# Mask and row maxima in one VectorE pass, and a new operation list with less work on GpSimd, in a fused attention and two-layer kernel

## The chip, the cores and the metric

The program runs on one core of a Trainium2 chip. The metric is the device time of one execution in microseconds (us); the profile adds one traced execution. The engines are called PE (TensorE, with PEld for its weight loads), DVE (VectorE), ACT (ScalarE), POOL (GpSimd) and SP (SyncE, which here only issues DMAs). A matrix product runs on PE, everything around it on DVE, ACT and POOL, and each engine works through its own queue strictly in order.

## The reference

Three stages follow one another on 1536 tokens (2 batches of 768) of width 512. First an attention with 8 heads of 64: each query sees the keys within 15 positions and, over all positions, 24 block keys (the maximum over blocks of 32) with block means as values. Then a gated layer of width 1536 behind an RMS norm, and a layer of width 2048 with ELU.

```python
k_sum = k.reshape(B, H, nb, 32, D).max(axis=3)
v_sum = v.reshape(B, H, nb, 32, D).mean(axis=3)
scores_l = np.where(mask_l, scale * q @ k.T, -1e9)          # |i - j| < 16
scores_s = scale * einsum('bhsd,bhnd->bhsn', q, k_sum) + log(32)
a = softmax(concat([scores_l, scores_s]), eps=1e-9)
x = a @ concat([v, v_sum])
xn = x / rms(x) * rms_g
x = (silu(xn @ w_gate) * (xn @ w_val)) @ w_out
out = elu(x @ w_in) @ w_out2
```

## The kernel before

**Tiles.** Attention is cut into 12 head-wise "pairs" of query tiles, (batch, j) with j = 0 to 5; each covers 128 queries and yields two tiles, (b, j, h) with h = 0, 1, of 128 rows by 4 head pairs by 120 columns (96 window keys and 24 block keys). A tile goes through `scores` (PE), mask, row maxima, `exps` (ACT, four exponentials with row sums), `guard` (row sum + 1e-9), `invert`, `normalize`, `turn_e` (PE transposes), `copy_e` and `apply_v2` (PE). For the first four pairs (eight tiles) PE adds the mask itself (`premask`), the keys are copied with the scale in them (`copy_keys`), and DVE takes only the row maxima. For the other eight pairs (16 tiles) DVE first scales the scores and adds the mask (`add_mask`) and then takes the row maxima of the result (`row_max`), each over 128x480.

**Layers.** The token axis is cut in three blocks of 512. Products run on float pairs: a weight tile `ws_*` or `wd` and an activation are split into a rounded high part (`split_a`, `act_a`: a cast on ACT) and a low part (`split_b`, `act_b`: a subtraction), and each product takes three matmuls of 512 columns. The weights arrive packed; `convert_a`, `convert_l` and `convert_b` unpack them on ACT and DVE. Block 0 goes through both layers directly while attention for the other two blocks proceeds; blocks 1 and 2 then share a seven-product scheme (`up_product`, `down_product`), which fills the rest of the time.

**Order.** Nothing is scheduled at run time. `add` records each operation with the engines that may do it, and `PLAN` lists all operations in the order of issue: a number is four times the operation's place in the record plus the choice of engine. `TAGS` chooses PSUM banks. So the queue of each engine, and of the DMAs on SP, is written out by hand. Before the first scores PE runs dummy matmuls on zeros (`keep_warm`), some of which wait for a key tile to land.

**POOL** in the old list has 55 operations: masks and zeros, four roots (`root`), six `normalize`, three `copy_keys`, four copies of the block means into value windows (`repeat_v`), two `add_square`, and 24 `split_b` and five `act_b` of 128x512.

Of the kernel before, what the change touches and what calls it, by code (L numbers as in the profile page):

```python
# [20 lines left out]
P = 128  # L21
# [30 lines left out]
def fused_kernel(ctx: ExitStack, tc: tile.TileContext, q, k, v, w_gate, w_val, w_out, rms_g, w_in2, w_out2, out):  # L52
# [342 lines left out]
    def add_place(b, due, gap):  # L395
        add({ACT: 0.72, DVE: 0.6} if b == 0 else {ACT: 0.8, DVE: 0.85}, 0, due, place_v, b, r=[f"vm{b}" if b else f"vp{b}"], w=["va0#s"])
        for i in range(1, VA):
            add({POOL: 0.6, ACT: 0.52} if b == 0 else {POOL: 0.6}, 0, due + gap * i, repeat_v, i, r=["va0#s"], w=[f"va{i}#s"])
# [18 lines left out]
    def copy_keys(eng, b, t):  # L417
        factor = scale if b * NQ + t < PRE else 1.0
# [47 lines left out]
    def add_mask(b, t, var):  # L466
        nc.vector.scalar_tensor_tensor(
            T[f"e{b}_{t}"], T[f"s{b}_{t}"], scale, masks[var].unsqueeze(1).to_broadcast([P, NP, NK]), op0=ALU.mult, op1=ALU.add)
# [4 lines left out]
    def exps(b, t, pre):  # L473
        e = T[f"e{b}_{t}"]
        s, nm = T[f"s{b}_{t}"] if pre else e, T[f"nm{b}_{t}"]
        ss = new("ss", f"ss{b}_{t}", [P, NP])
        for pr in range(NP):
            nc.scalar.activation(  # L478
                out=e[:, pr, :], in_=s[:, pr, :], func=AF.Exp, bias=nm[:, pr:pr + 1],
                accum_out=ss[:, pr:pr + 1])  # L480

    def guard(b, t):
        ss = T[f"ss{b}_{t}"]
        nc.vector.tensor_scalar_add(ss, ss, 1e-9)
# [47 lines left out]
    def add_pair(b, j, due, tags):  # L532
# [4 lines left out]
        for t in (2 * j, 2 * j + 1):  # L537
            lo, hi, _ = window(t)
            if b * NQ + t >= MT:
                add_window(b, t, due - 3)  # L540
            near = [f"kT{b}_{x}" for x in range(lo // (2 * P), (hi - 1) // (2 * P) + 1)]
            add({POOL: 0.86, DVE: 0.45, ACT: 0.65}, 0, due, copy_keys, b, t,
                r=near + far, w=[f"ka{b}_{t}"], new=[("ka", f"ka{b}_{t}")])
# [9 lines left out]
        for h, n in enumerate(ns):  # L553
            at = due + 0.6 * h
            src = f"s{n}"
            if not pre:
                add(DVE, 0.56, at + 1.4, add_mask, b, f"{j}_{h}", mask_of(j), r=[f"s{n}", f"mask{mask_of(j)}"], w=[f"e{n}"])
                src = f"e{n}"
            add(DVE, 0.56, at + 1.9, row_max, b, f"{j}_{h}", src, r=[src], w=[f"nm{n}"], new=[("nm", f"nm{n}")])
            add(ACT, 1.43 if pre else 1.5, at + 2.6, exps, b, f"{j}_{h}", pre, r=[f"nm{n}"] + [f"s{n}", f"pm{n}"] * pre,  # L560
                w=[f"e{n}", f"ss{n}"], new=[("ss", f"ss{n}")])
            add(DVE, 0.13, at + 4, guard, b, f"{j}_{h}", w=[f"ss{n}"])
            add(DVE, 0.1, at + 4, invert, b, f"{j}_{h}", r=[f"ss{n}"], w=[f"rs{n}"], new=[("rs", f"rs{n}")])
            add({POOL: 0.94, DVE: 0.58, ACT: 1.14}, 0, at + 4.3, normalize,
# [22 lines left out]
    def add_square(eng, blk, cs, i):  # L587
        s = T[f"sq{blk}_{SQ[blk][0]}{i}"]
        (nc.gpsimd if eng == POOL else nc.vector).tensor_add(s, s, T[f"sq{blk}_{cs}{i}"])
# [61 lines left out]
    def add_norm(blk, lo, hi, due, tag):  # L651
# [5 lines left out]
        for n, cs in enumerate(SQ[blk]):  # L657
# [3 lines left out]
            if n >= n_sums:  # L661
                add({POOL: 1.28, DVE: 0.6}, 0, due + 0.6 * n, add_square, blk, cs, i, r=[sq], w=[first])
# [92 lines left out]
    def add_act(src, dst, due, tag="act"):  # L755
        h, l = dst + "h", dst + "l"
        add(ANY_SB, 0, due, act_a, src, dst, tag, r=[src], w=[h], new=[(tag, h)])
        add(ANY_2[1], 0, due + 0.6, act_b, src, dst, tag, r=[src, h], w=[l], new=[(tag, l)])
# [463 lines left out]
    def keep_warm(i):  # L1222
# [3 lines left out]
        for _ in range(WARM_LONG.get(i, 2)):  # L1226
# [6 lines left out]
    for i, at in enumerate(WARM_AT):  # L1233
        add(PE, 0.44, at, keep_warm, i, r=[f"kT0_{AFTER_K[i]}"] if i in AFTER_K else [], new=[(BANKS, f"warm{i}")])
# [245 lines left out]
```

## Time and profile before

| | us |
|---|---|
| median of 3 runs (591.71 to 592.02) | 591.72 |
| the profiled execution's own time | 592.67 |
| its span, first to last instruction | 591.0 |
| PE busy | 574.1 (97%) |
| DVE busy | 547.3 (93%) |
| ACT busy | 430.4 (73%) |
| POOL busy | 69.6 (12%) |

The profiled execution lasted 1.67 us longer than its span and 0.95 us longer than the median run. Busy times are unions of the instructions' intervals; neighbouring instructions overlap, so the time from one start to the next is shorter than the mean duration that a view prints.

### The profile page before, as it was taken

How to read it: one execution, taken by the hardware profiler on the slowest of the kernel's cores; microseconds unless marked ns; L12 is line 12 of the kernel's file. 1: busy time of each engine (PE TensorE's matmuls, PEld its weight loads, DVE VectorE, ACT ScalarE, POOL GpSimd, SP SyncE). 2: the span in 40 equal slices, each digit the busy share in tenths (PEclk: the TensorE clock that was granted, in tenths of full speed). 3: DMA queues.
4: the chain of work that ended last, by engine and by line, in shares of the span. 5: the costliest groups of instructions: out<-in, count | busy, mean ns of one | idle time of the engine just before them, and what ended most of it. 6: DMA issues, size and time to landing. Idle time of an engine off the chain costs nothing.

```text
span 591.0 us, 9948 instructions
## 1 busy us (share of the span) xinstructions
PE 574.1 (97%) x3366; PEld 467.6 (79%) x3366; DVE 547.3 (93%) x1049; ACT 430.4 (73%) x953; POOL 69.6 (12%) x89
## 2 busy tenths in 40 slices
PE   7799989999999999999999999999999999999997
PEld 3588768788877888888888888888888888888886
DVE  5999999999989988989998999999999999999993
ACT  3889978998988988646534456676666989788750
POOL 3326425024100031100000000000000000000000
PEclk9999999999999999999999999999999999999999
DMA  8888889988978977142134416324316552742202
GB/s 318 287 297 280 303 303 321 325 300 282 312 231 273 318 232 265 55 159 71 55 91 161 143 50 188 92 81 142 107 38 196 200 159 78 244 129 65 71 35 107
DMA packets 56051, 108.79 MB, mean 184 GB/s; under 512 B 6784, under 2 KB 19584, under 8 KB 56000
## 3 DMA queue, kind: packets, MB, share of 16 engines
q1 hardware_dynamic: 56000, 108.16, 56.2%
q8 instruction: 26, 0.43, 0.3%
q14 instruction: 25, 0.20, 0.1%
HBM read 79.82 MB, written 28.31 MB: 183 GB/s over the span
## 4 chain that ended last, share of the span: by engine, by line
PE 81%; DVE 9%; ACT 6%; issue 2%; DMA 1%; POOL 0%; DVEq 0%; ACTq 0%; POOLq 0%
PE acc L766 11%; PE B_1u L937 8%; PE ph L710 7%; PE C_1u L937 6%; PE A_1u L937 6%; PE B_2d L1116 6%; PE B_2u L937 6%; PE B_1d L1116 4%; PE C_2d L1116 4%; PE A_2d L1116 4%; PE C_2u L937 4%; PE A_2u L937 4%; PE C_1d L1116 3%; PE A_1d L1116 3%; PE pg L710 2%
## 5 line engine op out<-in xcount | busy, mean ns | idle before, releaser
L710 PE MATMUL ph<-xa,ws_i 128*128 128x512 f32 x192 | 48.0, 395 | 0.6 <-DVE ex L747 0.6
L937 PE MATMUL B_1u<-xh,w_1u 128*128 128x512 f32 x144 | 47.8, 391 | 0.0
L710 PEld LDWEIGHTS ph<-xa,ws_i 128*128 128x128 f32 x192 | 35.5, 188 | 8.8 <-DVE ex L747 1.0
L710 PE MATMUL pg<-xs,ws_g 128*128 128x512 f32 (+1 forms) x168 | 36.4, 364 | 0.7 <-DVE th L734 0.7
L1116 PE MATMUL B_2d<-td,wd 128*128 128x512 f32 x144 | 34.6, 389 | 0.0
L146 DVE TENSOR_TENSOR wd<-rd,wd 128x512 fp32r<-128x512 f32 x49 | 32.8, 684 | 0.2 <-ACT wd L135 0.2
L937 PE MATMUL C_1u<-xh,w_1u 128*128 128x512 f32 x96 | 32.8, 390 | 0.0
L710 PEld LDWEIGHTS pg<-xs,ws_g 128*128 128x128 f32 x168 | 28.1, 189 | 5.5 <-DVE th L734 0.9
L937 PE MATMUL A_1u<-xh,w_1u 128*128 128x512 f32 x96 | 32.3, 390 | 0.0
L135 ACT CAST wd<-rd 128x512 fp32r<-128x512 f32 x49 | 29.1, 621 | 4.1 <-PE B_2u L937 2.2
L937 PEld LDWEIGHTS B_1u<-xh,w_1u 128*128 128x128 f32 x144 | 27.0, 188 | 6.1 <-ACT h_1u L135 0.3
L937 PE MATMUL B_2u<-xh,w_2u 128*128 128x512 f32 x96 | 31.6, 389 | 0.0
L1116 PEld LDWEIGHTS B_2d<-td,wd 128*128 128x128 f32 x144 | 27.0, 188 | 5.6
L937 PE MATMUL B_1u<-xl,w_1u 128*128 128x512 f32 x72 | 28.1, 390 | 0.0
L1116 PE MATMUL B_1d<-td,wd 128*128 128x512 f32 x108 | 26.5, 389 | 0.0
L478 ACT ACTIVATE e<-e,nm 128x120 f32<-128x120 f32 x64 | 24.5, 387 | 1.7 <-DVE nm L471 1.6
L135 ACT CAST td<-z 128x512 fp32r<-128x512 f32 x28 | 17.1, 619 | 11.7 <-DVE z L1098 11.6
L1116 PE MATMUL C_2d<-td,wd 128*128 128x512 f32 (+1 forms) x102 | 24.5, 377 | 0.0
L1116 PE MATMUL A_2d<-td,wd 128*128 128x512 f32 x96 | 24.0, 389 | 0.0
L1116 PEld LDWEIGHTS B_1d<-td,wd 128*128 128x128 f32 x108 | 20.3, 188 | 4.2
L135 ACT COPY h_1u<-B_1u 128x512 f32<-128x512 f32 x21 | 12.3, 587 | 12.9 <-PE B_1u L937 12.9
L937 PE MATMUL C_2u<-xh,w_2u 128*128 128x512 f32 x64 | 21.5, 389 | 0.0
(547 smaller groups left out, 1777.2 us busy)
## 6 DMA issues: line engine op xcount, KB each, us to landing
st_i<-in_moe_w_in SPq DMA_DIRECT2D x16, 512.0 KB, 4.4
st_p<-in_moe_w_out SPq DMA_DIRECT2D x16, 512.0 KB, 4.9
st_v<-in_moe_w_val SPq DMA_DIRECT2D x12, 512.0 KB, 6.8
st_g<-in_moe_w_gate SPq DMA_DIRECT2D x12, 512.0 KB, 6.1
st_o<-in_moe_w_out SPq DMA_DIRECT2D x12, 512.0 KB, 5.7
kept_i<-raw_i SPq DMA_DIRECT2D x16, 256.0 KB, 4.3
kept_p<-raw_p SPq DMA_DIRECT2D x16, 256.0 KB, 4.4
va<-in_v SPq DMA_DIRECT2D x20, 192.0 KB, 5.8
```

Source lines behind the costliest of these rows:

```text
L135: nc.scalar.copy(out=out, in_=in_)
L146: (nc.gpsimd if eng == POOL else nc.vector).tensor_sub(out, a, b)
L478: nc.scalar.activation(out=e[:, pr, :], in_=s[:, pr, :], func=AF.Exp, bias=nm[:, pr:pr + 1], accum_out=ss[:, pr:pr + 1])
L710: nc.tensor.matmul(pt[:, i], wt[:, a, kk * P:(kk + 1) * P], xt[:, c, i], start=(kk == 0 and n == 0), stop=(kk == KM - 1 and n == 2))
L766: nc.tensor.matmul(acc, wt[:, a, cs], ot[e], start=(first and n == 0), stop=(last and n == 2))
L937: nc.tensor.matmul(pt, wt[:, a, cs], xt[e][:, kk], start=first and kk == n == 0, stop=kk == 1 and n == 2, skip_group_check=not first)
L1116: nc.tensor.matmul(pt[:, h], wt[:, a, cs], xt[:, e, h], start=first and n == 0, stop=last and n == 2 and h.stop == TB, skip_group_check=i ...
```

## The change

For the 16 tiles of the later eight pairs, `add_mask` and `row_max` become four `tensor_tensor_reduce` instructions, one for each head pair (128x120): each adds the mask to the scores, multiplies by -1, writes the negated result and puts its minimum into `nm`. `exps` then exponentiates -1 times what was written. The scale is now in the copied keys of all pairs. On POOL remain masks, zeros and roots, six `normalize` and one `copy_keys` of the early pairs, and it gets 11 of the 24 `guard`. The 24 `split_b`, five `act_b` and two `add_square` go to DVE, `repeat_v` goes to DVE (five) and ACT (one), and 12 copies and squares go from DVE to ACT. The dummy matmuls keep their number (22 of 512 columns) but come in 11 short operations instead of eight, one of which had eight matmuls in a row. `PLAN` and `TAGS` are new from the first number to the last (2819 operations instead of 2832), so all engines' queues and SP's order of DMAs change.

```diff
     def add_place(b, due, gap):
...
         for i in range(1, VA):
-            add({POOL: 0.6, ACT: 0.52} if b == 0 else {POOL: 0.6}, 0, due + gap * i, repeat_v, i, r=["va0#s"], w=[f"va{i}#s"])
+            add({DVE: 0.34, ACT: 0.52}, 0, due + gap * i, repeat_v, i, r=["va0#s"], w=[f"va{i}#s"])
...
     def copy_keys(eng, b, t):
-        factor = scale if b * NQ + t < PRE else 1.0
+        factor = scale
...
     def add_mask(b, t, var):
-        nc.vector.scalar_tensor_tensor(
-            T[f"e{b}_{t}"], T[f"s{b}_{t}"], scale, masks[var].unsqueeze(1).to_broadcast([P, NP, NK]), op0=ALU.mult, op1=ALU.add)
+        e, x, nm = T[f"e{b}_{t}"], T[f"s{b}_{t}"], new("nm", f"nm{b}_{t}", [P, NP])
+        for pr in range(NP):
+            nc.vector.tensor_tensor_reduce(
+                e[:, pr, :], x[:, pr, :], masks[var], -1.0, 3.0e38, ALU.add, ALU.min, nm[:, pr:pr + 1])
...
-                out=e[:, pr, :], in_=s[:, pr, :], func=AF.Exp, bias=nm[:, pr:pr + 1],
+                out=e[:, pr, :], in_=s[:, pr, :], func=AF.Exp, bias=nm[:, pr:pr + 1], scale=1.0 if pre else -1.0,
                 accum_out=ss[:, pr:pr + 1])
-    def guard(b, t):
+    def guard(eng, b, t):
         ss = T[f"ss{b}_{t}"]
-        nc.vector.tensor_scalar_add(ss, ss, 1e-9)
+        (nc.gpsimd if eng == POOL else nc.vector).tensor_scalar_add(ss, ss, 1e-9)
...
-            add({POOL: 0.86, DVE: 0.45, ACT: 0.65}, 0, due, copy_keys, b, t,
+            add({POOL: 0.86, DVE: 0.45, ACT: 0.65} if early else {DVE: 0.45, ACT: 0.65}, 0, due, copy_keys, b, t,
...
-            add(DVE, 0.13, at + 4, guard, b, f"{j}_{h}", w=[f"ss{n}"])
+            add({DVE: 0.13, POOL: 0.25}, 0, at + 4, guard, b, f"{j}_{h}", w=[f"ss{n}"])
...
-            add({POOL: 0.94, DVE: 0.58, ACT: 1.14}, 0, at + 4.3, normalize,
+            add({POOL: 0.94, DVE: 0.58, ACT: 1.14} if early else {DVE: 0.58, ACT: 1.14}, 0, at + 4.3, normalize,
...
-    def add_square(eng, blk, cs, i):
+    def add_square(blk, cs, i):
         s = T[f"sq{blk}_{SQ[blk][0]}{i}"]
-        (nc.gpsimd if eng == POOL else nc.vector).tensor_add(s, s, T[f"sq{blk}_{cs}{i}"])
+        nc.vector.tensor_add(s, s, T[f"sq{blk}_{cs}{i}"])
...
-        add(ANY_2[1], 0, due + 0.6, act_b, src, dst, tag, r=[src, h], w=[l], new=[(tag, l)])
+        add(ANY_2[0], 0, due + 0.6, act_b, src, dst, tag, r=[src, h], w=[l], new=[(tag, l)])
...
-        for _ in range(WARM_LONG.get(i, 2)):
+        for _ in range(2):
...
 PLAN = (
...
-WARM_AT = (3.4, 3.9, 4.0, 7.5, 8.5, 9.5, 10.5, 13.0)
-AFTER_K, WARM_LONG = {1: 0, 2: 2}, {1: 8}
+WARM_AT = (3.4, 3.9, 4.0, 7.5, 8.5, 9.5, 10.5, 13.0, 7.8, 8.0, 8.2)
+AFTER_K = {1: 0, 2: 2, 8: 0, 9: 1, 10: 1}
 ACT_B = 0
-LO_0, LO_1 = (1, 1, 1), 0
+LO_0, LO_1 = (0, 0, 0), 0
```

## Rows read from the trace of the kernel before

**Rows 1.** Windows of 15 us: busy time of each engine, granted clock, DMA share.
```profile
0.00:15.00 15.00, 10.86 (x74) 5.24 (x78) 8.19 (x25) 5.70 (x19) 4.70 (x29) 1.00 0.87 321
15.00:30.00 15.00, 11.53 (x257) 8.97 (x250) 14.39 (x41) 13.24 (x63) 5.90 (x8) 1.00 0.85 282
30.00:45.00 15.00, 13.88 (x205) 12.52 (x206) 14.85 (x36) 13.46 (x32) 3.44 (x4) 1.00 0.87 302
45.00:60.00 15.00, 14.34 (x93) 12.86 (x92) 14.93 (x30) 14.53 (x44) 9.34 (x10) 1.00 0.88 284
60.00:75.00 15.00, 13.86 (x143) 10.82 (x145) 14.59 (x24) 12.56 (x32) 7.93 (x7) 1.00 0.87 300
75.00:90.00 15.00, 13.27 (x109) 9.88 (x99) 13.61 (x27) 12.75 (x33) 2.34 (x3) 1.00 0.87 296
...
375.00:390.00 15.00, 15.00 (x68) 12.42 (x67) 15.00 (x27) 10.92 (x21) 0.00 (x0) 1.00 0.23 67
```
**Rows 2.** The page's chain that ended last, by engine.
```profile
PE 81%; DVE 9%; ACT 6%; issue 2%; DMA 1%; POOL 0%; DVEq 0%; ACTq 0%; POOLq 0%
```
**Rows 3.** Timeline of PE, 4 to 18 us: start, us, instruction, count, wait.
```profile
7.03 1.05 PE L1227 MATMUL warm<-idle_w 128*128 128x512 bf16 x2
...
8.16 3.00 PE L1227 MATMUL warm<-idle_w 128*128 128x512 bf16 x8
...
11.38 1.05 PE L462 MATMUL s<-ka,q 64*64 64x120 f32 x32
...
14.76 1.05 PE L462 MATMUL s<-ka,q 64*64 64x120 f32 x32 [1.65 <-DVE ka L143]
15.74 0.60 PE L1227 MATMUL warm<-idle_w 128*128 128x512 bf16 x2
```
**Rows 4.** Timeline of DVE: operations beside POOL's, and one like the first.
```profile
2.86 0.60 DVE L195 CAST mask_b<-mask 128x96 bf16<-128x96 f32 x1 [1.15 <-POOL mask L170]
...
3.56 0.28 DVE L195 CAST mask_b<-mask 128x96 bf16<-128x96 f32 x1
...
56.17 1.27 DVE L484 TENSOR_SCALAR ss<-ss 128x4 f32<-128x4 f32 x1
...
257.90 1.78 DVE L856 TENSOR_TENSOR y_t<-xT,xT 128x512 f32<-128x512 f32 x1
259.72 0.69 DVE L856 TENSOR_TENSOR y_t<-xT,y_t 128x512 f32<-128x512 f32 x1
```
**Rows 5.** Timeline of POOL, 55.5 to 58 us.
```profile
56.12 1.30 POOL L146 TENSOR_TENSOR ws_g<-raw_g,ws_g 128x512 fp32r<-128x512 f32 x1
```
**Rows 6.** Groups on POOL by form: count, busy us, mean ns, idle before.
```profile
L146 POOL TENSOR_TENSOR ws_g<-raw_g,ws_g 128x512 fp32r<-128x512 f32 x8 | 10.8, 1360 | 3.5 <-ACT ws_g L135 3.4
...
L146 POOL TENSOR_TENSOR ws_i<-raw_i,ws_i 128x512 fp32r<-128x512 f32 x2 | 2.6, 1294 | 3.8 <-ACT ws_i L135 3.8
...
L422 POOL TENSOR_SCALAR ka<-ksum 128x96 f32<-128x96 f32 x3 | 1.2, 413 | 0.0
```
**Rows 7.** Groups on DVE by form: count, busy us, mean ns, idle before.
```profile
L471 DVE TENSOR_REDUCE nm<-e 128x4 f32<-128x480 f32 x16 | 10.3, 649 | 0.0
L467 DVE SCALAR_TENSOR_TENSOR e<-s,mask 128x480 f32<-128x480 f32 x16 | 10.2, 653 | 0.9 <-PE s L462 0.9
...
L137 DVE COPY ka<-kT 128x320 f32<-128x320 f32 x4 | 1.3, 320 | 0.0
```
**Rows 8.** Timeline of DVE: neighbours of one kind, for the time from start to start.
```profile
20.07 1.22 DVE L471 TENSOR_REDUCE nm<-s 128x4 f32<-128x480 f32 x2
...
26.20 0.38 DVE L488 RECIPROCAL rs<-ss 128x4 f32<-128x4 f32 x2
...
576.91 1.29 DVE L146 TENSOR_TENSOR wd<-rd,wd 128x512 fp32r<-128x512 f32 x2
```
**Rows 9.** Timeline of ACT: exponentials of 128x120 with row sums.
```profile
13.19 0.36 ACT L478 ACTIVATE e<-s,nm 128x120 f32<-128x120 f32 x1 [1.87 <-DVE nm L471]
13.44 0.19 ACT L478 ACTIVATION_READ_ACCUMULATOR e<-s,nm 128x1 f32 x1
13.54 0.35 ACT L478 ACTIVATE e<-s,nm 128x120 f32<-128x120 f32 x1
```

More of the change, by code (lines that the diff above doesn't have):

```diff
@@ L395, in add_place @@
     def add_place(b, due, gap):
-        add({ACT: 0.72, DVE: 0.6} if b == 0 else {ACT: 0.8, DVE: 0.85}, 0, due, place_v, b, r=[f"vm{b}" if b else f"vp{b}"], w=["va0#s"])
+        add({ACT: 1.2, DVE: 1.15} if b == 0 else {ACT: 1.15, DVE: 0.85}, 0, due, place_v, b, r=[f"vm{b}" if b else f"vp{b}"], w=["va0#s"])
         for i in range(1, VA):
-            add({POOL: 0.6, ACT: 0.52} if b == 0 else {POOL: 0.6}, 0, due + gap * i, repeat_v, i, r=["va0#s"], w=[f"va{i}#s"])
+            add({DVE: 0.34, ACT: 0.52}, 0, due + gap * i, repeat_v, i, r=["va0#s"], w=[f"va{i}#s"])
     def window(t):
@@ L554, in add_pair @@
             at = due + 0.6 * h
[L555 to L559, printed above, removed]
+            if pre:
+                add(DVE, 0.56, at + 1.9, row_max, b, f"{j}_{h}", f"s{n}", r=[f"s{n}"], w=[f"nm{n}"], new=[("nm", f"nm{n}")])
+            else:
+                add(DVE, 0.78, at + 1.4, add_mask, b, f"{j}_{h}", mask_of(j), r=[f"s{n}", f"mask{mask_of(j)}"], w=[f"e{n}", f"nm{n}"],
+                    new=[("nm", f"nm{n}")])
             add(ACT, 1.43 if pre else 1.5, at + 2.6, exps, b, f"{j}_{h}", pre, r=[f"nm{n}"] + [f"s{n}", f"pm{n}"] * pre,
                 w=[f"e{n}", f"ss{n}"], new=[("ss", f"ss{n}")])
-            add(DVE, 0.13, at + 4, guard, b, f"{j}_{h}", w=[f"ss{n}"])
+            add({DVE: 0.13, POOL: 0.25}, 0, at + 4, guard, b, f"{j}_{h}", w=[f"ss{n}"])
             add(DVE, 0.1, at + 4, invert, b, f"{j}_{h}", r=[f"ss{n}"], w=[f"rs{n}"], new=[("rs", f"rs{n}")])
-            add({POOL: 0.94, DVE: 0.58, ACT: 1.14}, 0, at + 4.3, normalize,
+            add({POOL: 0.94, DVE: 0.58, ACT: 1.14} if early else {DVE: 0.58, ACT: 1.14}, 0, at + 4.3, normalize,
                 b, f"{j}_{h}", r=[f"rs{n}"], w=[f"e{n}"])
@@ L661, in add_norm @@
             if n >= n_sums:
-                add({POOL: 1.28, DVE: 0.6}, 0, due + 0.6 * n, add_square, blk, cs, i, r=[sq], w=[first])
+                add(DVE, 0.6, due + 0.6 * n, add_square, blk, cs, i, r=[sq], w=[first])
         y = f"{blk}{i}"
@@ L1233, in fused_kernel @@
     for i, at in enumerate(WARM_AT):
-        add(PE, 0.44, at, keep_warm, i, r=[f"kT0_{AFTER_K[i]}"] if i in AFTER_K else [], new=[(BANKS, f"warm{i}")])
+        add(PE, 0.55 if i in AFTER_K else 0.43, at, keep_warm, i, r=[f"kT0_{AFTER_K[i]}"] if i in AFTER_K else [], new=[(BANKS, f"warm{i}")])
     add_vsum(0, VS0, VS0 + MEAN, BANKS)
@@ L1274 @@
 PLAN = (
[151 rows of a table removed]
[150 rows of a table added]
 )
 TAGS = (
-    "5431670427554360163402637014263701703011001010011010100010101011001111010110100110101011010100110101"
-    "0100110110111202111122030251200046070134100202103225102171002142073026102530400711020076203251304120"
-    "0210200274121131530212712021120023160220475012011000202625221020003227246522021111002742110122203507"
-    "0022221200322001"
+    "2010303227655137432176032472012350137101200111010101010101010101100100101110010010110011001010101010"
+    "1011100111101100101201030050010206010017216401321221040111220240576202121010560111042500371111605012"
+    "2240320131241270025306072100210213122640172000115222002600010530111047231562102072202130141020070031"
+    "2412003101000321022"
 )
```

301 rows, old and new, of the table PLAN are left out of this document.

## The prediction

> **What bounds the kernel.** I read first the windows of 15 us over the whole span, then the chain of waits, then the timelines of the head and of GpSimd, then the groups on POOL and DVE. The windows say where time can come from [rows 1]: from 90 us on PE is busy in nearly every microsecond, and the window from 375 us stands for that stretch. In the first six windows PE is idle for 4.14 + 3.47 + 1.12 + 0.66 + 1.14 + 1.73 = 12.3 us. The page counts 574.1 us of PE work in a span of 591.0, so 16.9 us are idle in all; the other 4.6 lie in short gaps later and behind the last product. The chain agrees: 81% of it is PE, 9% DVE and 6% ACT [rows 2]. So a faster operation somewhere else is worth something only if it brings PE's work forward in the first 90 us, and the change can give back at most those 12.3 us and some 2 us of dummy matmuls.
>
> What holds PE back there is mostly DVE. From 15 to 75 us it is busy for 14.39 + 14.85 + 14.93 + 14.59 = 58.8 of 60 us, while ACT over 15 to 90 us is idle for 75 - 66.5 = 8.5 us [rows 1]. In the window from 375 us DVE and PE are both full, 15.00 of 15. So later too DVE has no room: a longer DVE list would push the end out, a shorter one cannot pull it in by itself, because PE is full as well.
>
> **GpSimd slows DVE.** The timelines of both engines, laid over each other, show what GpSimd does to DVE. The guard of a 128x4 tile takes 1.27 us at 56.17 [rows 4], beside a POOL addition that runs from 56.12 for 1.30 us [rows 5]; two reciprocals of the same size take 0.38 us together [rows 8]. A 128x512 product takes 1.78 us at 257.90 and the next one 0.69 [rows 4]. There are 24 such DVE operations beside a POOL operation, from the mask cast at 2.86 (0.60 against 0.28 us) to the product at 257.90, and together they last 15.1 us longer than their like: 8.3 us up to 95 us, 6.8 after. The POOL operations beside them are chiefly the subtractions of about 1.3 us [rows 6], and those all go. Six early normalizes, one key copy and the setup remain; of the 24 cases I leave 1.5 us to them. The ends are 0.9 us (the casts at the head alone) and 6 us (each of the six normalizes stretching one operation by 1 us). Term: **-13.6 us** of DVE time.
>
> **What DVE gains and loses in work.** I count by time from start to start, since neighbours overlap. Two 128x512 subtractions take 1.29 us [rows 8], one alone 0.69 [rows 4], so one more costs 0.60. Two row maxima of 480 columns take 1.22 with a mean of 0.65 [rows 7, 8], so one more costs 0.57.
> Added: 24 `split_b`, five `act_b` and two `add_square`, 31 x 0.60 = 18.7 us; five `repeat_v` at about 0.34, like a copy of 128x320 with a mean of 0.32 [rows 7], 1.7 us. Together +20.4.
> Moved to ACT: 12 copies, squares and seeds of 128x512, 7.2 us; two small root copies, one normalize and one key copy, 1.7; less two weight casts that come to DVE, 0.7. The 11 guards that go to POOL cost at most 0.19 each (half of the pair in [rows 8]), 2.1 in all, and at least nothing where they hide behind a neighbour; I take 0.8. Together -9.0.
> The mask pass: 16 tiles lose two passes of 0.57, 1.13 us, and get four reduces of 128x120. No row shows one. A quarter of a 480-column pass each, with no start cost, is 0.14, or 0.57 per tile. A straight line between the small operation (0.19 for 4 columns) and the row maximum (0.57 for 480) gives 0.28, or 1.13, and no gain. Since half of a pair overstates a small operation's pitch, I take a value nearer the quarter, 0.195 each, 0.78 per tile: 16 x 0.35 = 5.6 us less, with ends of 9.0 and 0.
> DVE's work in sum: 20.4 - 9.0 - 5.6 = **+5.8 us**, so with the stretching gone DVE's list becomes 7.8 us shorter, not longer.
>
> **The head.** The first scores start at 11.38, behind eight dummies in a row that run from 8.16 to 11.16 [rows 3]. In the new list no operation has more than two dummies in a row, and several wait for key tiles, so the first scores follow the keys, whose copy on DVE I place near 9.6 us. The second key copy waits for DVE and holds the next scores until 14.76, with 1.65 us of idle PE ahead of it [rows 3]; it too comes earlier in the new list. Since the remaining dummies stand between, I take **-1.5 us**, with ends of 0 (the key tile lands no earlier and dummies fill the same time) and 2.5. POOL now writes zeros before the masks, which costs the mask casts half a microsecond; nothing on the path needs the masks for DVE until the fifth pair.
>
> **What is added to the path.** ACT's list grows by 7.6 us, mostly in the stretch where it had 8.5 us of idle time. If all its idle time is usable, this costs nothing; if none is, 7.6. Exponentials stand in its queue behind any copy that waits, and PE's transposes wait for them through `normalize`. I charge a third, 2.4 us, in which the guards on POOL are included: each makes ss go from ACT to POOL to DVE, and `invert` behind it on DVE holds all that is queued there, but in 10 of the 11 cases other DVE operations stand between. An 11-fold stall of 0.41 us, the mean of the only small POOL operations [rows 6], would be 4.5. Term: **+2.4 us**.
>
> **The sum.** -13.6 + 5.8 - 1.5 + 2.4 = -6.9 us, which the 12.3 us of idle PE can take in: for the eased DVE in the first 95 us alone I have 8.3 us of stretching, most of the reduce's 5.6 and the head. The span becomes 584.1. The profiled execution lasts 1.67 us longer than its span and was 0.95 over the median, so the median becomes 584.1 + 1.67 - 0.95 = **584.8 us**. With the bounds of the terms this is 582 to 588.5: the reduce moves it by -3.4 or +5.6, contention that stays by up to +4.5, ACT by -2.4 or +5.2, and they will not all fall on one side.
>
> **Rivals.**
> *The reduce is two instructions each (the slower side).* ACT's exponential with a row sum is followed by a second instruction that fetches the sum; from one exponential's start to the next are 13.54 - 13.19 = 0.35 us for the same 128x120 [rows 9]. If DVE does the same at that price, a tile costs 1.40 instead of 0.78, 16 x 0.62 = 9.9 us more, on an engine that is full: 594.7 us. It decides from 1.21 us per tile on (6.9/16 = 0.43 above 0.78), 0.30 per instruction. For it speaks that ss and nm are built alike; against it that DVE's own row maximum shows no second record [rows 8]. Chance 0.10. The Trainium skill ("VectorE: DVE Perf Modes", section "Two Vector instructions with no wait between them") says that a Vector operation that also writes its accumulator out is two instructions, the main one and an accumulator read; the trace of before shows this on ACT only [rows 9]. By that rule the time would come out between my sum and 594.7.
> *ACT becomes the bound.* All 7.6 us of its new work come onto the path instead of 2.4: 590.0. It speaks for it that ACT too is busy for 66.5 of 75 us in the stretch that matters; against it the 8.5 us left. Chance 0.08.
> *The relief is off the path.* DVE's stretched operations were waiting for nothing that PE needed, and PE starts no sooner: 590 to 591.7, the dummies alone giving up to 1.5. Against it: DVE is 98% busy between 15 and 75 us. Chance 0.07.
> *PE starts slower.* Two dummies take 1.05 us at 7.03 and 0.60 at 15.74, both at a granted clock of 1.00, the level of 2.4 GHz, in the windows [rows 1, 3]. Against it, the scores at 11.38 and 14.76 take 1.05 alike. With shorter runs of dummies the faster rate may come later, and the first products lose 2 to 3 us: 587 to 588. Chance 0.07.
> *Nearly all idle PE time goes.* 10 of the 12.3 us and 2 us of dummies: 580. For it speaks that POOL was also a producer of PE's operands, so that waits for its 1.3 us subtractions go too; against it that the head's 4.14 us hold the loading of the first tiles. Chance 0.12.
>
> **Numbers.** My forecast, 582 to 588.5, has the remaining 0.56. About 0.2% (1.2 us) is what a measurement of this kernel can tell from no change, so the bound for faster is 590.5. Faster: 0.56 + 0.07 + 0.12 and half of ACT's 0.08, 0.79. Same: the other half and most of the hidden relief, 0.08. Slower: the two-instruction reduce and the rest, 0.13. The range from 579.5 to 592.0 leaves out half of the lowest case and the slower one.
>
> **What would show it.** Right: no DVE operation of 128x4 beyond 0.5 us and no 128x512 beyond 1 us behind the early normalizes; 64 reduces at 0.19 us from start to start; first scores before 10.5 us; PE idle near 5 us in the first six windows; POOL busy below 25 us. Wrong: reduces with a second record, or above 0.30 from start to start; ACT without idle time from 15 to 90 us and named ahead of PE's waits; DVE full and PE not, behind 345 us, which would mean that the +5.8 us weigh more than the stretching that went.

## The result and the profile after

| | before | after |
|---|---|---|
| median (4 runs each) | 591.87 us | 583.74 us (583.21 to 584.44) |
| ratio, 95% interval | | 0.9857 (0.9837 to 0.9878) |
| span of the profiled execution | 591.0 | 581.5 |
| PE busy | 574.1 | 573.3 |
| DVE busy | 547.3 | 540.1 |
| ACT busy | 430.4 | 436.6 |
| POOL busy | 69.6 | 21.5 |

The change takes 8.1 us off, against the 6.9 forecast (584.8 us). First the windows of 15 us of the kernel after, which answer to [rows 1] (time, then busy time of PE, PEld, DVE, ACT and POOL with counts, granted clock, DMA share, GB/s):

```profile
0.00:15.00 15.00, 12.19 (x109) 6.69 (x110) 9.08 (x29) 6.85 (x25) 6.10 (x34) 1.00 0.88 323
15.00:30.00 15.00, 13.39 (x272) 9.99 (x271) 14.79 (x48) 14.59 (x62) 5.53 (x9) 1.00 0.95 308
30.00:45.00 15.00, 14.72 (x183) 13.56 (x180) 14.95 (x56) 15.00 (x43) 4.25 (x6) 1.00 1.01 340
45.00:60.00 15.00, 15.00 (x141) 13.21 (x144) 14.25 (x29) 14.87 (x41) 1.12 (x4) 1.00 0.95 314
60.00:75.00 15.00, 15.00 (x121) 11.99 (x110) 14.63 (x41) 15.00 (x35) 0.22 (x1) 1.00 0.94 305
75.00:90.00 15.00, 15.00 (x124) 11.98 (x123) 14.78 (x43) 14.75 (x44) 0.80 (x2) 1.00 0.98 338
...
375.00:390.00 15.00, 15.00 (x68) 12.41 (x67) 14.96 (x25) 11.03 (x21) 0.00 (x0) 1.00 0.43 128
```

PE is idle for 2.81 + 1.61 + 0.28 = 4.70 us in the first 90, where it was 12.26 [rows 1]: 7.56 us back. Two later windows of before had 0.51 and 0.56 us of idle PE, and after they have none: 1.07.

```profile
105.00:120.00 15.00, 14.49 (x124) 11.69 (x123) 13.90 (x28) 13.85 (x29) 1.29 (x1) 1.00 0.97 309
165.00:180.00 15.00, 14.44 (x117) 11.20 (x116) 13.12 (x24) 11.99 (x24) 2.25 (x3) 1.00 0.84 272
```

PE's own busy time is 0.84 us shorter. Together 9.5 us, which is the whole difference of the two spans (591.0 - 581.5); the tail behind the last product is unchanged. DVE is as full as it was (58.6 of 60 us from 15 to 75), and ACT has lost nearly all its idle time there: 75 - 74.21 = 0.8 us from 15 to 90, where it was 8.5. So three engines are full at once now, PE from 45 us on. The page's chain of waits, which answers to [rows 2], says the same:

```profile
PE 95%; DVE 2%; ACT 2%; DMA 1%; issue 0%; ACTq 0%
```

The new mask pass, in the timeline of DVE (start, us, instruction):

```profile
29.40 0.27 DVE L469 CUSTOM_DVE_ANT_0 e<-s,mask 128x120 f32<-128x120 f32 x1
29.60 0.08 DVE L469 DVE_READ_ACCUMULATOR2_ANT nm<- 128x1 f32 x1
29.60 0.27 DVE L469 CUSTOM_DVE_ANT_0 e<-s,mask 128x120 f32<-128x120 f32 x1
29.80 0.08 DVE L469 DVE_READ_ACCUMULATOR2_ANT nm<- 128x1 f32 x1
```

Each reduce is two instructions, as the first rival said: the main one and a read of the accumulator. But the second starts in the same moment as the next main one, so the pair costs 0.20 us from start to start, and a tile 0.81. On ACT the like pair costs 0.35 [rows 9].

The head, in the timeline of PE, which answers to [rows 3]:

```profile
8.85 0.66 PE L1229 MATMUL warm<-idle_w 128*128 128x512 bf16 x2
9.77 1.05 PE L462 MATMUL s<-ka,q 64*64 64x120 f32 x32 [0.26 <-issue]
...
13.52 1.05 PE L462 MATMUL s<-ka,q 64*64 64x120 f32 x32
```

The first scores start at 9.77 instead of 11.38, the second at 13.52 instead of 14.76, without a wait for keys. Of POOL's groups [rows 6] remain six normalizes and the 11 guards, besides setup, roots and one key copy:

```profile
L495 POOL TENSOR_TENSOR e<-e,rs 128x480 f32<-128x480 f32 x6 | 6.1, 1038 | 7.5 <-DVE rs L490 4.4 <-PE at L505 3.0
L486 POOL TENSOR_SCALAR ss<-ss 128x4 f32<-128x4 f32 x11 | 3.7, 334 | 80.5 <-ACT e L480 80.3
```

DVE operations that last longer beside a POOL operation than their like: three, with 0.5 us in all, where there were 24 with 15.1 us [rows 4].

### The profile page after: what moved, and what is told of

It reads as the page before. It is cut to its first block, busy times and chain, and to the rows that moved or that the text cites. A ratio compares the mean times of both kernels' runs of the same rounds, so it can differ in the third digit from the quotient of the medians.

```text
span 581.5 us, 10057 instructions
## 1 busy us (share of the span) xinstructions
PE 573.3 (99%) x3372; PEld 468.3 (81%) x3372; DVE 540.1 (93%) x1154; ACT 436.6 (75%) x975; POOL 21.5 (4%) x61
## 4 chain that ended last, share of the span: by engine, by line
PE 95%; DVE 2%; ACT 2%; DMA 1%; issue 0%; ACTq 0%
PE acc L768 13%; PE B_1u L939 8%; PE ph L712 8%; PE pg L712 6%; PE C_1u L939 6%; PE B_2d L1118 6%; PE B_2u L939 6%; PE A_1u L939 6%; PE B_1d L1118 4%; PE C_2d L1118 4%; PE A_2d L1118 4%; PE C_2u L939 4%; PE A_2u L939 4%; PE C_1d L1118 3%; PE A_1d L1118 3%; PE pv L517 2%
## 5 line engine op out<-in xcount | busy, mean ns | idle before, releaser
L712 PE MATMUL ph<-xa,ws_i 128*128 128x512 f32 x192 | 46.7, 394 | 0.0
L135 ACT COPY h_1u<-B_1u 128x512 f32<-128x512 f32 x21 | 12.3, 587 | 17.2 <-PE B_1u L939 14.8
```

The lines of the kernel that those rows point to most:

```text
L135: nc.scalar.copy(out=out, in_=in_)
L712: nc.tensor.matmul(pt[:, i], wt[:, a, kk * P:(kk + 1) * P], xt[:, c, i], start=(kk == 0 and n == 0), stop=(kk == KM - 1 and n == 2))
```

## Experiments

Every step of the prediction's sum was tried twice where that could be done: alone in the old list, and taken back out of the new one. Beside these runs the kernel before had medians of 591.8 to 592.0 us.

| run | median us | ratio to before, 95% |
|---|---|---|
| b_dve: old list, 31 operations from POOL to DVE | 596.04 | 1.0060 (1.0038 to 1.0081) |
| b_ttr: old list, new mask pass | 590.73 | 0.9980 (0.9969 to 0.9991) |
| b_both: old list, both | 593.76 | 1.0023 (1.0004 to 1.0041) |
| b_act: old list, 13 copies to ACT | 593.84 | 1.0032 (1.0021 to 1.0043) |
| b_all: old list, all three edits | 598.00 | 1.0099 (1.0080 to 1.0118) |
| the change | 583.74 | 0.9857 (0.9837 to 0.9878) |
| a_pool: change, 31 operations back on POOL | 586.93 | 0.9920 (0.9900 to 0.9941) |
| a_old: change, two passes again | 584.80 | 0.9878 (0.9861 to 0.9894) |
| a_act: change, 13 copies back on DVE | 595.86 | 1.0068 (1.0053 to 1.0083) |
| a_guard: change, guards on DVE | 584.05 | 0.9877 (0.9860 to 0.9893) |
| a_warm8: change, dummies ahead of the first scores | 585.96 | 0.9901 (0.9887 to 0.9916) |
| a_nowarm: change, those dummies left out | 586.28 | 0.9925 (0.9898 to 0.9951) |
| a_dup: change, idle work on POOL | 588.63 | 0.9948 (0.9934 to 0.9963) |

**b_dve, the subtractions on DVE in the old list.**

```diff
     def minus(eng, out, a, b):
-        (nc.gpsimd if eng == POOL else nc.vector).tensor_sub(out, a, b)
+        nc.vector.tensor_sub(out, a, b)
...
-        (nc.gpsimd if eng == POOL else nc.vector).tensor_add(s, s, T[f"sq{blk}_{cs}{i}"])
+        nc.vector.tensor_add(s, s, T[f"sq{blk}_{cs}{i}"])
```

> The old list with one edit: its 24 split_b, five act_b and two add_square run on DVE where they stood, nothing else moves. My theory (GpSimd beside DVE stretches DVE, 15.1 us in 24 operations): DVE gets 31 x 0.60 = 18.6 us of work and loses about 14 of stretching, net +4 to +5 on an engine that is full, so 593 to 597 us, and no DVE operation over 1 us is left behind the early normalizes. Rival one (the stretching was time in which DVE would have waited anyway): +10 to +18.6, 602 to 610. Rival two (the 1.3 us that a GpSimd subtraction takes was what PE waited for): below 590.

596.0 us, 4.1 slower, where the sum gave +4 to +5. The stretching is 2.7 us instead of 15.1, and DVE's busy time grows by 6.6 us (547.3 to 553.9). Both rivals fall. But part of the 4.1 us is PE's clock: the four runs lie between 594.4 us with a mean granted clock of 1.000 and 598.3 with 0.988, and in the profiled one, the slowest of them, the clock fell at four places. One of them, in windows of 3 us:

```profile
81.00:84.00 3.00, 0.76 (x4) 0.64 (x4) 2.90 (x6) 3.00 (x6) 0.00 (x0) 0.97 1.03 412
84.00:87.00 3.00, 3.00 (x9) 2.33 (x8) 3.00 (x7) 2.90 (x13) 1.43 (x3) 0.50 0.33 86
```

By the one run with 1.000 the edit costs some 2.5 us, less than the sum gave.

**b_ttr, the mask pass in the old list.** `copy_keys`, `add_mask` and `exps` as in the change, and

```diff
     def row_max(b, t, src):
+        if src[0] == "e":
+            return
```

> The old list with the new mask pass alone (scale in all copied keys, four reduces per tile, no separate maxima). The trace after shows 0.81 us per tile against 1.13, so 16 x 0.32 = 5.1 us of DVE time go. My theory (DVE sets PE's pace until 90 us, and later both are full): a gain of 2 to 5, 587 to 590 us. Rival (the pass is hidden in the old list, where other waits end last): 591 to 592.

590.7 us, 1.2 faster. DVE's busy time falls by 5.1 us (547.3 to 542.2), as the time from start to start says, but a quarter of that reaches the end.

**b_both**, the two edits together.

> The old list with both edits, the 31 operations on DVE and the new mask pass. My theory: both act on one full engine and add up, net DVE time -14 + 18.6 - 5.1, about 0, so 590 to 593 us, and what the change gained beyond that is the new list's (the work moved to ACT, and the head). Rival (the two edits are the whole gain and the new order only goes with them): 584 to 587.

593.8 us, 1.8 slower, where the two effects add up to 2.9. So in the old order the two edits together gain nothing; the change's gain needs more than them.

**a_pool, the subtractions back on POOL in the new list.**

```diff
     def split_b(eng, ws, raw, cs):
         t = T[ws]
+        eng = POOL if ws in ON_POOL else eng
...
     def act_b(eng, src, dst, tag):
+        eng = POOL if dst in ON_POOL else eng
...
     def add_square(blk, cs, i):
...
-        nc.vector.tensor_add(s, s, T[f"sq{blk}_{cs}{i}"])
+        (nc.gpsimd if late else nc.vector).tensor_add(s, s, T[f"sq{blk}_{cs}{i}"])
```

`ON_POOL` names the 29 tiles of the old list, `late` its two sums.

> The new list with the same 31 operations put back on GpSimd where they stand. My theory: DVE loses 18.6 us of work, but 8 to 15 us of stretching come back, and PE's operands come 0.7 us later each: 585 to 592 us, slower than the change. Rival (DVE's length alone counts): DVE 18.6 us shorter, PE gets back what it still waits, 579 to 582.

586.9 us, 3.2 slower than the change. The stretching is back at 20.5 us in 27 operations. DVE, then POOL, in their timelines of this run:

```profile
74.18 1.69 DVE L146 TENSOR_TENSOR act_1l<-th,act_1h 128x512 fp32r<-128x512 f32 x1 [1.27 <-ACT act_1h L135]
75.80 1.78 DVE L146 TENSOR_TENSOR ws_o<-raw_o,ws_o 128x512 fp32r<-128x512 f32 x1
```
```profile
74.03 1.29 POOL L146 TENSOR_TENSOR act_2l<-th,act_2h 128x512 fp32r<-128x512 f32 x1
75.29 1.74 POOL L146 TENSOR_TENSOR ws_v<-raw_v,ws_v 128x512 fp32r<-128x512 f32 x1
```

In both places DVE's operation, of a kind that takes 0.69 us alone, ends 0.55 us after POOL's, and POOL's second takes 1.74 us instead of 1.29: where they overlap, each holds the other up. In the old list DVE's taking these operations cost 4.1 us, in the new one DVE's giving them up costs 3.2: the same edit has the other sign.

**a_old, two passes in the new list.**

```diff
-        for pr in range(NP):
-            nc.vector.tensor_tensor_reduce(
-                e[:, pr, :], x[:, pr, :], masks[var], -1.0, 3.0e38, ALU.add, ALU.min, nm[:, pr:pr + 1])
+        nc.vector.tensor_tensor(e, x, masks[var].unsqueeze(1).to_broadcast([P, NP, NK]), op=ALU.add)
+        row_max(b, t, f"e{b}_{t}")
```

> The new list with the old two passes in the place of the four reduces: mask added over 128x480, then the row maxima, back to back. DVE gets 16 x 0.32 = 5.1 us more. My theory (DVE is full from 15 to 90 us in the new list too, 14.3 to 14.9 of each 15): most of it arrives, 586 to 588.5 us. Rival (ACT, which is as full now, or the order of the list sets the pace; the old list gave only 1.2 for the pass): 584 to 585.

584.8 us, 1.1 slower with intervals that overlap, though DVE has 5.2 us more (545.3): the rival's number. So the mask pass is worth a quarter of the DVE time that it saves in the old list, and in the new one at most a little more than a fifth, which is not clear of noise.

**a_dup, POOL made busy with nothing.**

```diff
+    junk = const.tile([P, P], F32, name="junk")
+    def extra(a, b):
+        for n in range(3):
+            nc.gpsimd.tensor_sub(junk, a[:, P * n:P * n + P], b[:, P * n:P * n + P])
...
     def split_b(eng, ws, raw, cs):
         t = T[ws]
+        if ws in ON_POOL:
+            extra(T[raw].bitcast(F32), t[:, 0].bitcast(F32))
```

and the same ahead of the five `act_b`.

> The new list unchanged, with three subtractions of 128x128 on GpSimd, into a scrap tile that nobody reads, ahead of each of 29 of DVE's subtractions (those that the old list gave to GpSimd). No operand comes from them and DVE's list is the same. My theory (GpSimd running beside DVE is itself the cost): DVE operations stretched by 8 to 20 us in sum, 587 to 594 us. Rival (what cost time in the old list were late operands and waits for GpSimd, not the running beside each other): 583 to 585.

588.6 us, 4.9 slower, though nothing waits for what the added POOL operations compute; the waits of the other engines for POOL are those of the change, within 0.4 us in all. DVE and POOL in their timelines:

```profile
53.04 0.95 DVE L275 SCALAR_TENSOR_TENSOR raw_g<-st_g 128x512 uint32<-128x512 uint32 x1
53.92 0.95 DVE L146 TENSOR_TENSOR ws_v<-raw_v,ws_v 128x512 fp32r<-128x512 f32 x1
...
62.14 0.71 DVE L749 SCALAR_TENSOR_TENSOR th<-th,pv_2c 128x512 f32<-128x512 f32 x1
62.74 0.71 DVE L749 SCALAR_TENSOR_TENSOR th<-th,pv_0c 128x512 f32<-128x512 f32 x1
```
```profile
52.47 2.72 POOL L308 TENSOR_TENSOR junk<-raw_v,ws_v 128x128 f32<-128x128 f32 x3
...
62.30 0.99 POOL L308 TENSOR_TENSOR junk<-raw_g,ws_g 128x128 f32<-128x128 f32 x2
```

In all, DVE operations last 13.1 us longer than their like, about 0.27 us each at most, since the POOL operations are now short. This shows the contention by itself. The two at 62.14 and 62.74 are not stretched beside POOL's subtractions: one of their two inputs, `pv`, lies in PSUM. That is the rule of the Trainium skill ("SBUF — State Buffer", section "Who interferes with whom"), by which a DVE instruction with two inputs in SBUF contends with a GpSimd instruction that reads SBUF, and one with at most one such input does not, outside of the two-port modes. The trace agrees in these rows.

**a_act, 13 copies and squares back on DVE.**

```diff
     def copy_e(eng, b, t):
+        eng = DVE if ("copy_e", b, t) in ON_DVE else eng
```

and the same in `copy_x2` and `square`: six, five and two operations, named in `ON_DVE`.

> The new list, with 13 copies and squares of 128x512 that the change moved to ACT back on DVE, in their places: DVE 7.8 us longer, ACT about 7 us shorter. My theory (DVE's length sets the pace in the first 90 us and ACT's idle time was free to use): 586 to 591. Rival (ACT is now the bound, the charge that I made for it was too small): below 583.7.

595.9 us, 12.1 slower, for 7.6 us more DVE time: the greatest effect of any part, and beyond my range. One place, PE and then DVE in their timelines:

```profile
25.80 0.62 PE L505 MATMUL at<-ident,e 128*120 128x128 f32 x4
27.84 1.15 PE L522 MATMUL pv<-ats,va 120*64 120x64 f32 x32 [1.42 <-DVE ats L137]
```
```profile
25.66 0.71 DVE L279 SCALAR_TENSOR_TENSOR raw_v<-st_v,raw_v 128x512 uint16<-128x512 uint16 x1
26.41 0.69 DVE L137 COPY xT<-pv 128x512 f32<-128x512 f32 x1
27.02 0.68 DVE L137 COPY ats<-at 120x512 f32<-120x512 f32 x1
```

PE waits 1.42 us for a copy that stands on DVE behind a weight's unpacking and another copy. In the new list ACT does it at 24.64, and PE starts `pv` at 25.48 with no wait:

```profile
24.64 0.71 ACT L135 COPY ats<-at 120x512 f32<-120x512 f32 x1
```
```profile
25.48 1.15 PE L517 MATMUL pv<-ats,va 120*64 120x64 f32 x32
```

A second loss comes from the clock. Windows of 3 us of a_act from 33 us, columns as above:

```profile
33.00:36.00 3.00, 1.49 (x10) 0.85 (x9) 1.59 (x10) 3.00 (x8) 0.61 (x1) 1.00 0.95 343
36.00:39.00 3.00, 2.95 (x62) 2.64 (x62) 3.00 (x7) 1.06 (x3) 0.00 (x0) 0.64 0.67 236
39.00:42.00 3.00, 3.00 (x17) 2.91 (x14) 3.00 (x8) 2.80 (x11) 0.61 (x1) 0.50 0.97 365
42.00:45.00 3.00, 3.00 (x21) 3.00 (x20) 3.00 (x14) 3.00 (x7) 0.42 (x1) 0.73 1.00 295
```

PE was half idle from 33 to 36 us; then the granted clock falls to 0.50, the level of 1.2 GHz, and comes back before 45. 3 x (0.36 + 0.50 + 0.27) = 3.4 us of PE's time are lost in this stretch to the clock. The change has 1.00 up to its last product. That the half-idle stretch brought the fall about is not shown: from 108 to 111 us of the same execution PE was busy for 1.48 of 3 us, and the clock stayed at 1.00.

In all, the span is 12.3 us longer than the change's. PE is busy for 4.2 us more, 3.4 of which are this clock, and idle for 3.5 us more in the first 90 us and 4.6 more behind them, most of it from 105 to 120 us, where it waits again for a copy moved to DVE:

```profile
114.84 1.15 PE L522 MATMUL pv<-ats,va 120*64 120x64 f32 x32 [1.79 <-DVE ats L137]
```

**b_act and b_all, the same copies on ACT in the old list**, alone, and with the other two edits (and the repeated block means on DVE).

> The old list with the 13 copies and squares moved to ACT in their old places and nothing else: DVE 7.8 us shorter, ACT some 6.5 us longer. Taken back from the new list they cost 12.1 us. If what counts is the sum on DVE: 584 to 588. If what counts is where a copy stands in a queue (the old list placed them for DVE): 588 to 593.

593.8 us, 2.0 slower, though DVE is 6.6 us shorter (540.7, like the change's 540.1) and ACT as long as in the change (437.0 and 436.6). PE in the timeline of before, then in that of b_act:

```profile
28.81 1.15 PE L515 MATMUL pv<-ats,va 120*64 120x64 f32 x32 [3.02 <-DVE ats L137]
```
```profile
26.03 1.15 PE L520 MATMUL pv<-ats,va 120*64 120x64 f32 x32 [0.76 <-ACT ats L135]
...
32.93 1.15 PE L520 MATMUL pv<-ats,va 120*64 120x64 f32 x32 [0.16 <-ACT ats L135]
...
35.54 1.15 PE L520 MATMUL pv<-ats,va 120*64 120x64 f32 x32 [0.47 <-ACT ats L135]
...
38.96 0.42 PE L462 MATMUL s<-ka,q 64*64 64x120 f32 x4 [1.30 <-issue]
```

The old kernel's wait of 3.02 us for a copy on DVE is gone, and three for ACT of 1.4 us in all have come, where copies stand behind exponentials (eight with their reads, 2.7 us) and casts. What ended the 1.30 us ahead of 38.96 the profile does not name. Yet over the first 90 us PE is idle for 11.22 us, less than the 12.26 of before. What b_act loses lies behind: 2.89 us of idle PE from 90 to 255 us, against 1.07. That makes its span 0.8 us longer; the rest of the 2.0 us between the medians these two executions do not show.

> The old list with the 31 operations and the repeated block means on DVE, the new mask pass, and the 13 copies and squares on ACT: every edit of the change that moves more than 2 us of work, but in the old order and with the old head. By the sum of work: 593.8 - 7.8 and some of ACT's growth, 586 to 588. If the order is what the gain needs: 590 to 594. The head alone (2.2 us by the run before) would make 585.9 of the new list.

598.0 us. This is the sharpest of the runs. It has all the edits that move over 2 us of work, its DVE has 542.4 us of work and its ACT 437.0, within 2.3 us of the change, its stretching is 1.2 us, and it takes 14.3 us more than the change. PE is idle for 12.46 us in its first 90, as in the kernel before (12.26), where the change has 4.70. About 3.3 us more of PE's time go to the clock, which falls twice:

```profile
78.00:81.00 3.00, 1.26 (x8) 0.84 (x6) 3.00 (x7) 3.00 (x6) 0.00 (x0) 1.00 1.05 420
81.00:84.00 3.00, 2.86 (x7) 2.28 (x8) 2.90 (x9) 2.92 (x10) 0.00 (x0) 0.57 0.47 187
...
123.00:126.00 3.00, 1.31 (x9) 1.09 (x9) 2.14 (x5) 2.88 (x7) 0.00 (x0) 0.97 0.53 216
126.00:129.00 3.00, 3.00 (x9) 2.32 (x8) 2.50 (x4) 2.78 (x5) 1.56 (x1) 0.50 0.43 100
```

What b_all lacks is the new order: the new `PLAN`, with the head and smaller choices of engine (the guards among them).

**a_guard.** All 11 guards on DVE: `nc.vector.tensor_scalar_add(ss, ss, 1e-9)` for either engine.

> The new list with its 11 guards on DVE instead of GpSimd. My theory (they cost DVE little and their way over GpSimd is hidden): between -0.5 and +1 us, 583.2 to 584.7. Rival (each hand-over holds the reciprocal on DVE for 0.2 us and more): 580 to 582.5.

584.05 us, 0.3 above the change, with intervals that overlap. The guards' move cannot be told from nothing.

**a_warm8 and a_nowarm, the dummies.** A count for each operation in `keep_warm`, two where none is given:

```diff
-        for _ in range(2):
+        for _ in range({1: 10, 10: 0, 8: 0, 9: 0, 0: 0}.get(i, 2)):
```

> The new list, with the eight dummy matmuls that stood behind the first scores moved ahead of them, so that ten run in a row there as eight did in the old list. First scores 1.7 to 2 us later than 9.77. My theory (the head is on the path): 584.8 to 586. Rival (the head is hidden behind DVE's or the DMAs' own pace): 583.3 to 584.3.

586.0 us, 2.2 slower. The first scores start 1.9 us later than in the change (9.77), and this arrives whole:

```profile
11.66 1.05 PE L462 MATMUL s<-ka,q 64*64 64x120 f32 x32
```

In a_nowarm the eight dummies are left out, with no entry for 1:

> The new list without the eight dummy matmuls behind the first scores (1.7 to 2.3 us of PE time between 10.7 and 15.5). My theory (they fill idle time, at most 0.6 us of them stands ahead of the second scores): 582.9 to 583.9. Rival (they hold PE's clock: without them the granted clock falls in the first 20 us): above 585. Rival (they hold PE up): below 582.5.

586.3 us, 2.5 slower, my theory's number missed. The second scores do start earlier, 12.67 instead of 13.52, but PE is idle for 9.53 us in the first 90, where the change has 4.70, and in the profiled execution, the slowest of the seven, the clock falls again:

```profile
36.00:39.00 3.00, 1.71 (x20) 1.55 (x16) 3.00 (x9) 3.00 (x13) 0.00 (x0) 0.87 1.00 382
39.00:42.00 3.00, 3.00 (x15) 3.00 (x16) 3.00 (x13) 3.00 (x9) 0.57 (x1) 0.50 1.03 322
42.00:45.00 3.00, 3.00 (x16) 3.00 (x16) 3.00 (x12) 3.00 (x12) 1.42 (x2) 0.50 1.00 336
```

Its runs lie between 585.3 us with a mean clock of 1.000 and 590.7 with 0.993, so part of the loss is the clock, and it does not come in every execution. The run at 1.000 is still 1.6 us slower than the change; what the dummies are good for, beside the clock, stays open.

## Why the prediction was right, and which step of it was not

**Right in result and in most terms.** 584.8 was forecast, 583.74 measured. The stretching of DVE went from 15.1 to 0.5 us, 14.6 against the term of 13.6. DVE's busy time fell by 7.2 us against 7.8 expected, ACT's grew by 6.2 against 7.6. A reduce tile takes 0.81 us against 0.78, so the pass gives 5.1 us of DVE time against 5.6. The first scores start at 9.77 (near 9.6 expected); a_warm8 prices the head at 2.2 us, against 1.5 with an end of 2.5. PE's idle time is 4.7 us, near the 5 named as a sign. Of the signs named for a wrong forecast, the reduce's second record came, and ACT was left with hardly any idle time from 15 to 90 us; neither brought the price that I had put on it. 31 x 0.60 is 18.6, not 18.7, which changes nothing.

**The two-instruction rival** was right in mechanism and wrong in price. The Trainium skill ("VectorE: DVE Perf Modes", section "Two Vector instructions with no wait between them") says that such an operation is a main instruction and an accumulator read, and the trace agrees: 64 reads of 0.08 us. Each starts together with the next main one, so they add little: a tile takes 0.81 us, near the 0.78 that I had put on the four main ones alone. No run has the reduce without its read, so that the read costs nothing at all is not shown. ACT's pair [rows 9] was the wrong row to price it by.

**What failed is the step from DVE's list to the end:** "with the stretching gone DVE's list becomes 7.8 us shorter", which idle PE "can take in". That step sets 1 us of DVE equal to 1 us of the end, wherever it lies; even the 6.8 us of stretching behind 95 us are in it, where PE, ahead of its last product, was idle for only 1.07 us. The runs show no such rate. 6.6 us less DVE gave 2.0 us more time (b_act), 5.1 less gave 1.2 less (b_ttr), 5.2 more gave 1.1 more (a_old), and 7.6 more gave 12.1 more (a_act). b_all has nearly the change's work on every engine and is slower than before. So the terms of the sum were well sized, but the gain is not their sum. With nearly the same work PE is idle for 12.46 us of the first 90 in the old order and 4.70 in the new one. I read this so that the edits made room and the new order turned it into earlier PE work; no run has the new order alone. I held the new order for a carrier of the edits, with 1.5 us for its head; against b_all it and the smaller choices that go with it are worth 14.3 us, some 3.3 of them by way of the clock. That -6.9 was so near is then partly luck: the same kind of sum gave 586 to 588 us for b_all, which took 598.0.

**ACT.** I charged 2.4 us for its growth, by a share of its idle time. It filled all of that idle time, 8.5 to 0.8 us, and PE has only short waits for it. The rival in which ACT becomes the bound, at 590.0 us, is refuted for this order. In the old one the same moves cost 2.0 us, but behind 90 us PE waits there for DVE and POOL as well as for ACT, so whether ACT is the bound there stays open.

**The other rivals** did not come. PE does not start slower: two dummies take 0.66 us at 8.85, the first scores 1.05 us as before. And of the 12.26 us of idle PE in the first 90, 7.56 went and not 10.

**Contention.** Its size was right, and a_dup and a_pool show the cause itself. But removing it by moving the work to DVE was no gain in the old order (+4.1 us, +2.5 in the run at full clock).

**The clock.** I took the granted clock as given, 1.00 throughout. In the profiled executions of a_act, a_nowarm and b_all it fell to the level of 1.2 GHz for a while, and PE lost 3.4, 3.2 and 3.3 us by it (its busy time times what the clock lacked); in those of b_dve, b_ttr and b_both too, with 6.4, 1.6 and 1.6 us. Each fall came in or right behind a stretch in which PE was partly idle, but not each such stretch was followed by one: in the kernel before, PE was busy for 2.98 of the 6 us from 24 us on, and the clock stayed at 1.00. What decides it is not shown. It is a term that a sum of engine times does not have, and part of why some steps cost more than their work, added to the old list or taken out of the new one.

**Not settled:** how the 14.3 us divide between the order as such, the smaller choices of engine and the head. The order was not varied by itself.

## What to carry to other kernels

Where several engines are full at once and each has a hand-written queue, the busy time of an engine tells what room there is, not what an edit is worth; test the edit in the old order and its undoing in the new one, and be ready for different signs, as with the subtractions here. A copy that PE waits for belongs on the engine where little stands ahead of it, even if that engine's copy is no faster: the one at 24.64 us took 0.71 us on ACT, as good as the 0.68 on DVE, and came 2.4 us sooner. GpSimd was no free help for VectorE where both read SBUF: for the 18.6 us that it took off DVE's list it took back 12.4 in stretched operations (15.1 in the kernel before, 2.7 in b_dve).

## What was not expected of the hardware

The read of a reduce's accumulator on DVE (0.08 us) starts with the next main instruction, so that four pairs and their reads take 0.81 us; ACT's reads start 0.10 us ahead of its next exponential, and a pair takes 0.35 us [rows 9]. And PE's clock fell to 0.50 for some 6.8 us in the a_act and a_nowarm executions, behind or at the end of 3 us in which PE was busy for 1.49 and 1.71, though over the span it is busy for 97 or 98%; in a_act it did not fall after another 3 us with 1.48.
